# Loading K and V of four heads of B: one DMA of 128 partitions in place of four DMAs of 32

## The chip, the cores and the metric

The kernel runs on one core of a Trainium2 chip. The metric is device time in microseconds (us). Before: 829.31 us, median of 3 runs (829.16 to 829.46). Runs of a kernel on one core are called fast when they are within 1.5% of its fastest; every time and ratio below is of fast runs unless it says otherwise.

## The reference

Two attention problems, A and B, each with one query token, 32 heads of 128 channels and a cache of 16,384 keys in bf16. A attends to all keys; B only to the last 4,096. Both outputs go through an output projection and are concatenated. The code below is B's part, shortened.

```python
def _B_ref(x, k_cache, v_cache, wq, wo):        # A is the same with all Sk keys
    # ...
    W = min(4096, max(256, Sk // 4))
    q = ((x @ wq).reshape(B, Sq, Hq, Dh)).transpose(0, 2, 1, 3)
    k = k_cache[:, :, Sk - W:, :]                # one KV head per query head
    v = v_cache[:, :, Sk - W:, :]
    p = softmax(einsum("bhqd,bhkd->bhqk", q, k) * Dh ** -0.5)
    return einsum("bhqk,bhkd->bhqd", p, v) ... @ wo
```

A head of A has 4 MiB of K and 4 MiB of V. A head of B has 1 MiB of each, so four heads of B make a load as large as one of A. In device memory the heads of B's caches lie 4 MiB apart, since the cache holds all 16,384 keys.

## The kernel before

The unit of work is one head of A or four heads of B: 128 partitions of 128 keys each. In a unit of B, partition p holds keys of head p mod 4; the query and a mask are laid out to match. VectorE multiplies K by the query and adds halves, TensorE finishes the sum over channels and then applies the probabilities to V. Two K buffers and two V buffers are filled by DMAs that SyncE issues in one fixed order; a load is issued as soon as the last reader of its buffer is done. (Cuts are marked `# ...`.)

```python
cx.kt_pool = pool("kt", 2)
cx.vt_pool = pool("vt", 2)
# ...
units = []
for h in range(stA.H):
    units.append((stA, [h]))                               # one head of A
    if h % G == G - 1:
        units.append((stB, list(range(h - G + 1, h + 1)))) # four heads of B

def _load_kv(nc, cx, unit, which):
    pool, tag = (cx.kt_pool, "kt") if which == "k" else (cx.vt_pool, "vt")
    t = pool.tile([P, unit.keys, DH], BF16, tag=tag, name=tag)
    setattr(unit, tag, t)
    st = unit.st
    view = st.k_view if which == "k" else st.v_view
    n = len(unit.heads)                                    # 1 for A, 4 for B
    for g, h in enumerate(unit.heads):
        src = view[h].rearrange("(p l) d -> p l d", p=P // n)
        cx.o(nc.sync.dma_start(out=t[g:P:n, :, :], in_=src))
# ...
    if ch.last_of_unit:
        cx.loads.release("kt")      # after the multiply; V is released after its last matmul
```

The softmax here doesn't subtract the row's maximum and nothing guards it: scores larger than these inputs give would overflow.

Of the kernel before, what the change touches and what calls it, by code (L numbers as in the profile page):

```python
# [10 lines left out]
P = 128  # L11
# [132 lines left out]
# [5 lines that stand above are left out]
    st = unit.st  # L149
    view = st.k_view if which == "k" else st.v_view  # L150
    n = len(unit.heads)
    for g, h in enumerate(unit.heads):
        src = view[h].rearrange("(p l) d -> p l d", p=P // n)
        cx.o(nc.sync.dma_start(out=t[g:P:n, :, :], in_=src))  # L154


def _mult(nc, cx, ch):
# [160 lines left out]
def kernel(  # L318
# [144 lines left out]
    for i in range(n + 1):  # L463
        if i == G - 1:
            ld.add("kt", lambda: _load_wq(nc, cx, stB, "kt"))
        if i < n:
            ld.add("kt", lambda u=units[i]: _load_kv(nc, cx, u, "k"))
        if i:
            ld.add("vt", lambda u=units[i - 1]: _load_kv(nc, cx, u, "v"))
# [94 lines left out]
```

## Time and profile before

| | before |
|---|---|
| time, median | 829.31 us |
| span of the profiled execution | 827.4 us |
| bytes through the load queue | 352.33 MB |
| load queue, share of 16 engines | 99.2% |
| DVE, PE busy | 71%, 49% |
| packets under 512 B | 2,482 |
| issue of B's loads on SyncE | 64 issues, 0.587 us each (median) |

The span is the time of the profiled execution on the chip. In the views DVE is VectorE, PE is TensorE, SP is SyncE, and SPq is SyncE's own instruction queue, where it issues DMAs and waits. A packet is one piece that one DMA engine moves: here 10,496 of them are rows of 32 KB, and most of those under 512 B (2,226 of 2,482) are of 4 bytes, 9 ns each. They are called completions here: they come 16 to a DMA, as do the updates of the semaphore (the counter that reports a landing) of 139 of the 141 DMAs in the trace.

The first lines are from the page of the kernel before. "DMA" is the busy share of the 16 DMA engines in each of 40 slices of the span, in tenths; "GB/s" is what they moved in each slice; the line beginning q1 is the queue that carries all the loads.

```profile
DMA  9999999999999999999999999999999999999996
GB/s 380 437 430 432 433 430 432 431 431 432 431 429 436 432 430 430 431 433 433 432 429 430 429 431 432 432 432 430 431 430 430 429 431 432 431 432 433 431 423 290
DMA packets 13902, 352.69 MB, mean 426 GB/s; under 512 B 2482, under 2 KB 2484, under 8 KB 2868
...
q1 hardware_dynamic: 13588, 352.33, 99.2%
```

The engines never pause (99.2% busy), and they move 429 to 437 GB/s in every slice except the first and the last two. Slices with loads of B look like slices with loads of A. That is the main reading: this kernel waits for bytes. The median of the 40 slices is 431 GB/s.

Next, the chain of work that ended last, by engine and by line (shares of the span):

```profile
DMA 68%; DVE 20%; issue 9%; PE 1%; SPq 1%; ACT 0%; DVEq 0%
```

And the DMA issues of the loads (tile, source, engine and instruction, count, size of each, median us from issue to landing), from the same page:

```profile
kt<-in_A_k_cache_dram SPq DMA_DIRECT2D x32, 4096.0 KB, 27.1
...
kt<-in_B_k_cache_dram SPq DMA_DIRECT2D x32, 1024.0 KB, 23.7
vt<-in_B_v_cache_dram SPq DMA_DIRECT2D x32, 1024.0 KB, 22.5
```

4,096 KB take 9.7 us to move, yet 27.1 us pass from issue to landing. The difference, some 17 us, is mostly the queue of loads that stands in front. The timeline of SyncE shows how much of its time a load of B takes (start, duration, line, tile and source, count):

```profile
269.24 2.39 SPq L154 DMA_DIRECT2D kt<-in_B_k_cache_dram  x4
276.63 0.34 SPq L154 DMA_DIRECT2D vt<-in_A_v_cache_dram  x1
288.66 0.33 SPq L154 DMA_DIRECT2D kt<-in_A_k_cache_dram  x1
```

The trace also holds one record per DMA packet, with its start, its duration and its size. Cutting those records at every 4 MiB of landed bytes gives the time of each load while the queue is full; this table is worked out from them (medians, the first five and last few loads left out):

| us per 4 MiB | A, K | A, V | B, K | B, V |
|---|---|---|---|---|
| before | 9.716 | 9.719 | 9.727 | 9.726 |

### The profile page before, as it was taken

The numbers are of one execution on the slowest core, as the hardware profiler recorded it, in microseconds if no ns is written. First come the engines' busy times: TensorE is split into PE (matmuls) and PEld (weight loads), VectorE is DVE, ScalarE is ACT, GpSimd is POOL, SyncE is SP. The second block draws the span as 40 slices with busy tenths as digits, with TensorE's granted clock in tenths as the row PEclk, the third lists the DMA queues.
The fourth block names the chain that finished last, engine by engine and source line by source line (L and its number), as shares of the span: only waits on it lengthen the run. The fifth ranks groups of instructions, "written<-read, shape, count | busy, mean of one in ns | idle before, by whom it ended". The sixth has DMA issues, their size and how long they took to land.

```text
span 827.4 us, 5769 instructions
## 1 busy us (share of the span) xinstructions
PE 403.7 (49%) x2368; PEld 138.7 (17%) x2368; DVE 584.7 (71%) x286; ACT 68.1 (8%) x301; POOL 4.5 (1%) x17
## 2 busy tenths in 40 slices
PE   3356444434555544554454445445455455544355
PEld 1112111111211111211121111111111111211123
DVE  2892777777777777766777777777777776777760
ACT  2000011000100001000110001100010000100010
POOL 2000000000000000000000000000000000000000
PEclk9778677666776668766686666766677766676779
DMA  9999999999999999999999999999999999999996
GB/s 380 437 430 432 433 430 432 431 431 432 431 429 436 432 430 430 431 433 433 432 429 430 429 431 432 432 432 430 431 430 430 429 431 432 431 432 433 431 423 290
DMA packets 13902, 352.69 MB, mean 426 GB/s; under 512 B 2482, under 2 KB 2484, under 8 KB 2868
## 3 DMA queue, kind: packets, MB, share of 16 engines
q1 hardware_dynamic: 13588, 352.33, 99.2%
q8 instruction: 18, 0.29, 0.1%
q14 instruction: 8, 0.07, 0.0%
q10 hardware_dynamic: 288, 0.00, 0.0%
HBM read 352.32 MB, written 0.00 MB: 426 GB/s over the span
## 4 chain that ended last, share of the span: by engine, by line
DMA 68%; DVE 20%; issue 9%; PE 1%; SPq 1%; ACT 0%; DVEq 0%
DMA kt<-in_A_k_cache_dram 49%; DVE prod L161 12%; DMA kt<-in_B_k_cache_dram 12%; DVE half L173 6%; DMA wq_t<-in_B_wq_dram 3%; DMA woB<-in_B_wo_dram 3%; DMA vt<-in_B_v_cache_dram 2%; DVE sc L203 2%; SPq L154 1%; PE q_ps L123 1%; PE red L186 0%; PE acc L233 0%; ACT qallB L130 0%; DVEq L161 0%; DVE recip L267 0%
## 5 line engine op out<-in xcount | busy, mean ns | idle before, releaser
L186 PE MATMUL red<-half,ident 128*128 128x512 bf16 x640 | 253.3, 567 | 388.1 <-DVE half L173 374.4
L161 DVE TENSOR_TENSOR prod<-kt,qallA 128x8192 bf16<-128x8192 bf16 x64 | 283.2, 4426 | 159.8 <-DMA kt<-in_A_k_cache_dram 159.1
L173 DVE TENSOR_TENSOR half<-prod 128x4096 bf16<-128x4096 bf16 x80 | 182.5, 2282 | 0.0
L186 PEld LDWEIGHTS <-ident 128*128 128x128 bf16 x640 | 81.8, 128 | 535.3 <-issue 508.1
L161 DVE TENSOR_TENSOR prod<-kt,qallB 128x8192 bf16<-128x8192 bf16 x16 | 70.8, 4426 | 40.3 <-DMA kt<-in_B_k_cache_dram 40.1
L233 PE MATMUL acc<-vt,pA 128*16 128x512 bf16 x1024 | 89.4, 484 | 0.1
L210 ACT ACTIVATE pA<-sc 128x64 bf16<-128x64 f32 x64 | 16.4, 256 | 518.3 <-DVE sc L203 518.3
L203 DVE TENSOR_REDUCE sc<-red 128x64 f32<-128x512 f32 x80 | 54.7, 684 | 3.4 <-PE red L186 3.3
L233 PEld LDWEIGHTS <-pA 128*16 128x16 bf16 x1024 | 22.9, 100 | 73.2 <-issue 66.8
L210 ACT ACTIVATE p_sb<-sc,off 128x64 bf16<-128x64 f32 x64 | 21.5, 336 | 92.1 <-DVE sc L203 92.1
L257 PE MATMUL f_ps<-acc_sb,sel 128*4 128x128 f32 x128 | 16.6, 273 | 10.7 <-ACT acc_sb L244 10.7
L233 PE MATMUL acc<-vt,p_sb 128*16 128x512 bf16 x256 | 20.5, 450 | 0.2 <-DMA vt<-in_B_v_cache_dram 0.2
L244 ACT COPY acc_sb<-acc 128x512 f32<-128x512 f32 x16 | 9.4, 585 | 79.3 <-PE acc L233 79.3
L123 PE MATMUL q_ps<-wq_t,xbA 128*128 128x512 bf16 x32 | 8.5, 431 | 13.2 <-DMA wq_t<-in_A_wq_dram 13.2
L257 PEld LDWEIGHTS f_ps<-acc_sb,sel 128*4 128x4 f32 x128 | 9.8, 86 | 14.5 <-ACT acc_sb L244 12.3
L210 ACT ACTIVATION_READ_ACCUMULATOR pA<-sc 128x1 f32 x64 | 11.9, 187 | 0.0
L210 ACT ACTIVATION_READ_ACCUMULATOR p_sb<-sc,off 128x1 f32 x64 | 11.9, 187 | 0.0
L123 PE MATMUL q_ps<-wq_t,xbB 128*128 128x512 bf16 x32 | 7.2, 379 | 2.3 <-DMA wq_t<-in_B_wq_dram 1.6
L233 PEld LDWEIGHTS <-p_sb 128*16 128x16 bf16 x256 | 5.4, 95 | 15.6 <-issue 13.1
L269 ACT ACTIVATE orow<-f_ps,recip 4x128 bf16<-4x128 f32 x16 | 5.7, 358 | 20.5 <-DVE recip L267 20.5
L95 DVE COPY xbB<-xTB 128x32 bf16<-128x32 bf16 x16 | 1.5, 199 | 8.1 <-DMA xTB<-in_B_x_dram 8.1
L267 DVE RECIPROCAL recip<-f_ps 4x1 f32<-4x1 f32 x16 | 2.4, 150 | 6.0 <-PE f_ps L257 6.0
(35 smaller groups left out, 53.6 us busy)
## 6 DMA issues: line engine op xcount, KB each, us to landing
kt<-in_A_k_cache_dram SPq DMA_DIRECT2D x32, 4096.0 KB, 27.1
vt<-in_A_v_cache_dram SPq DMA_DIRECT2D x32, 4096.0 KB, 29.6
kt<-in_B_k_cache_dram SPq DMA_DIRECT2D x32, 1024.0 KB, 23.7
vt<-in_B_v_cache_dram SPq DMA_DIRECT2D x32, 1024.0 KB, 22.5
wq_t<-in_A_wq_dram SPq DMA_DIRECT2D x1, 4096.0 KB, 12.4
wq_t<-in_B_wq_dram SPq DMA_DIRECT2D x1, 4096.0 KB, 23.8
woA<-in_A_wo_dram SPq DMA_DIRECT2D x2, 2048.0 KB, 29.3
woB<-in_B_wo_dram SPq DMA_DIRECT2D x1, 2048.0 KB, 23.6
```

The costliest lines, as they stand in the source:

```text
L123: cx.o(nc.tensor.matmul(q_ps[:, :], lhsT=st.xb[:, c, g, :], rhs=w[:, g, j * (512 // DH) : (j + 1) * (512 // DH), :], start=(g == 0 and c = ...
L154: cx.o(nc.sync.dma_start(out=t[g:P:n, :, :], in_=src))
L161: cx.o(nc.vector.tensor_tensor(out=ch.prod[:, :, :], in0=u.kt[:, ch.k0 : ch.k0 + U, :], in1=q.rearrange("p (o d) -> p o d", o=1).broadcast ...
L173: cx.o(nc.vector.tensor_tensor(out=ch.half[:, :, :], in0=ch.prod[:, :, 0 : DH // 2], in1=ch.prod[:, :, DH // 2 : DH], op=ALU.add,))
L186: cx.o(nc.tensor.matmul(ch.red[:, :, :], lhsT=cx.ident[:, :], rhs=ch.half[:, :, b * W : (b + 1) * W], start=(b == 0), stop=(b == nb - 1),))
L203: cx.o(nc.vector.tensor_reduce(out=sc[:, :], in_=ch.red[:, :, :], axis=AX.X, op=ALU.add))
L210: cx.o(nc.scalar.activation(out=ch.p[:, :, g, :], in_=sc[:, :].rearrange("p (t e) -> p t e", e=4), func=ACT.Exp, scale=SCALE, bias=0.0 if ...
L233: cx.o(nc.tensor.matmul(gr.acc[r : r + 4 * G, :], lhsT=ch.p[:, t, :, :], rhs=u.vt[:, k : k + 4, :], start=(first and t < 4), stop=(last an ...
L244: cx.o(nc.scalar.copy(gr.acc_sb[:, :], gr.acc[:, :]))
L257: cx.o(nc.tensor.matmul(gr.f_ps[:, 0:DH], lhsT=cx.sel[:, e, :], rhs=gr.acc_sb[:, e * DH : (e + 1) * DH], start=False, stop=(e == 3), skip_ ...
L267: cx.o(nc.vector.reciprocal(recip[:, :], gr.f_ps[:, DH : DH + 1]))
L269: cx.o(nc.scalar.activation(out=gr.orow[:, :], in_=gr.f_ps[:, 0:DH], func=ACT.Copy, scale=recip[:, 0:1]))
```

## The change

The intent is one large DMA over 128 partitions in place of several small ones, with fewer issues on SyncE and fewer completions on the engines. The destination is the same tile in the same layout. The source becomes three-dimensional: 32 blocks of 32 KB, for each block the 4 heads, 4 MiB apart.

```diff
-    for g, h in enumerate(unit.heads):
-        src = view[h].rearrange("(p l) d -> p l d", p=P // n)
-        cx.o(nc.sync.dma_start(out=t[g:P:n, :, :], in_=src))
+    src = view[unit.heads[0] : unit.heads[0] + n].rearrange("g (i l) d -> i g l d", i=P // n)
+    cx.o(nc.sync.dma_start(out=t[:, :, :], in_=src[:, 0, :, :] if n == 1 else src))
```

## The prediction

> **What bounds the kernel now.** The DMA engines, by bytes. The page's queue table has the load queue busy for 99.2% of 16 engines' span (827.4 us), moving 352.33 MB; the slices show about 430 GB/s throughout. The chain of waits is 68% DMA; DVE is busy 71%, PE 49%. In the trace's packet records nearly everything is a 32 KB packet, one partition row of a load (10,496 of them): median 1.215 us. Priced at the shortest, 1.213 us, all bytes take 815 us on 16 engines. The first packet starts 2.0 us into the span, the last ends 1.4 us before its end. So a rearrangement of loads can win under 9 us (about 1%), and most of that is the start and the end.
>
> **Are the B loads slower now?** No. Cutting the packet records at every 4 MiB, a whole-head load of A takes 9.71 to 9.72 us (median), a four-DMA load of B 9.726 us: 0.01 us more, for 16 loads, so 0.2 us in the kernel.
>
> **What the change removes.** 64 DMAs become 16. Packets under 512 B are 2,482 now; 16 per DMA are completion writes, so 48 x 16 = 768 go, leaving about 1,714. One is 9 ns: 768 x 9 / 16 = 0.43 us at most. On SyncE, four issues take 2.39 us in the timeline, one about 0.33 to 0.6 us; but from issue to landing a load takes 27 us (median) for 9.7 us of transfer, so some 17 us of other loads stand in front, and an earlier issue only stands longer in the queue. Bytes, row length, buffers, and the order of work on PE, DVE and ACT stay.
>
> **What it adds or moves.** The DRAM side gets three dimensions: 32 blocks of 32 KB, 4 heads 4 MiB apart. [...]
>
> **On the critical path:** 0.2 to 0.4 us.
>
> **Predicted time:** 829.0 us, 827.0 to 832.0 us eight times in ten. Faster by over 2%: 0.01. Within 2%: 0.94. Slower by over 2%: 0.05.
>
> **What would show it.** Right: 32 KB packets still 10,496 with median 1.215 us; packets under 512 B near 1,714; load queue at 99%; GB/s slices level; B loads at 9.71 to 9.73 us per 4 MiB; from issue to landing of B's loads 25 to 29 us; fewer issues on SyncE.
>
> **What would make it wrong.** (1) The source is cut differently: shorter packets, or unequal rows per engine, seen as more packets or slices dipping where B is loaded. (2) [...] 32 KB packets above 1.3 us. B's loads are 67 of 352 MB, about 156 us, so packets 10% longer cost 16 us, twice as long 156 us. (3) Issuing the new form takes SyncE over 10 us and drains the queue. Nothing I see makes it faster by 2%: the bytes forbid it.

0.2 to 0.4 us off the 829.31 us before came to 829.0 us. The 16 and 156 us under (2) are estimates from the 156 us that B's loads take.

## The result

| | before | after |
|---|---|---|
| time, median of 6 | 829.26 us (829.05 to 829.46) | 829.13 us (828.85 to 829.23) |
| ratio after to before | | 0.9998, 95% interval 0.9985 to 1.0011 |
| load queue, share | 99.2% | 99.1% |
| packets under 512 B | 2,482 | 1,714 |
| SyncE issues of B's loads | 64 of 0.587 us | 16 of 0.547 us |
| DVE idle for K of B | 40.1 us | 39.9 us |

Ratios here are the mean time of one kernel's fast runs over the mean of the other's of the same rounds, so they are not quite the ratio of the medians. The time is the same. The lines of the page after that answer to those of before:

```profile
DMA  9999999999999999999999999999999999999996
GB/s 380 434 430 432 432 432 435 431 432 430 434 429 434 430 431 430 434 431 426 434 432 430 429 431 430 431 432 432 432 430 431 429 431 433 431 433 431 432 423 285
DMA packets 13133, 352.68 MB, mean 426 GB/s; under 512 B 1714, under 2 KB 1716, under 8 KB 2100
...
q1 hardware_dynamic: 12820, 352.33, 99.1%
```

Exactly 768 packets are gone, 16 for each of the 48 DMAs saved. Bytes and rate are the same. What VectorE waited for K of B (us, times), before and then after:

```profile
  DMA kt<-in_B_k_cache_dram: 40.1, 8
```

```profile
  DMA kt<-in_B_k_cache_dram: 39.9, 8
```

The DMA issues after:

```profile
kt<-in_A_k_cache_dram SPq DMA_DIRECT2D x32, 4096.0 KB, 27.0
...
kt<-in_B_k_cache_dram SPq DMA_DIRECT2D x8, 4096.0 KB, 27.0
vt<-in_B_v_cache_dram SPq DMA_DIRECT2D x8, 4096.0 KB, 29.6
```

A reader could take 27.0 us after 23.7 us for a loss. It is not: before, the figure is the median of four pieces of 1 MiB, after, it is of the whole 4 MiB. What VectorE waited for K of B in all, 40.1 and 39.9 us, hardly changed.

SyncE's timeline around the same load shows the saving, 0.55 us in place of 2.39:

```profile
269.33 0.55 SPq L153 DMA_DIRECT2D kt<-in_B_k_cache_dram  x1
276.70 0.34 SPq L153 DMA_DIRECT2D vt<-in_A_v_cache_dram  x1
288.75 0.33 SPq L153 DMA_DIRECT2D kt<-in_A_k_cache_dram  x1
```

The next two issues start 0.07 and 0.09 us later than before, not 1.84 us earlier. SyncE's own waits say why. First the kernel before, then after (who waited for what, us in total, times, longest):

```profile
SPq L154 <- DVE prod L161: 417.1, 37, 12.0
SPq L154 <- PE acc L233: 221.6, 36, 7.9
```

```profile
SPq L153 <- DVE prod L160: 428.9, 37, 11.8
SPq L153 <- PE acc L232: 235.0, 36, 7.9
```

SyncE spends 16 x 1.84 = 29.4 us less on issuing and 11.8 + 13.4 = 25.2 us more on waiting for buffers. The time saved on issues became waiting.

Per 4 MiB, from the packet records, A's loads take 9.715 to 9.716 us, B's 9.712 (K) and 9.713 (V). By these medians B's loads gained 0.015 and 0.013 us each, 0.22 us for all 16; by the means of the same loads they gained 0.007 and 0.005 us, 0.1 us in all. Both are within the scatter of the run times.

### The profile page after: what moved, and what is told of

Same layout as the page of the kernel before. It is cut to its first block, busy times and chain, and to the rows that moved or that the text cites. A ratio compares the mean times of both kernels' runs of the same rounds, so it can differ in the third digit from the quotient of the medians.

```text
span 827.4 us, 5697 instructions
## 1 busy us (share of the span) xinstructions
PE 402.1 (49%) x2368; PEld 139.4 (17%) x2368; DVE 584.8 (71%) x286; ACT 68.2 (8%) x301; POOL 4.6 (1%) x17
## 2 busy tenths in 40 slices
DMA packets 13133, 352.68 MB, mean 426 GB/s; under 512 B 1714, under 2 KB 1716, under 8 KB 2100
## 3 DMA queue, kind: packets, MB, share of 16 engines
q1 hardware_dynamic: 12820, 352.33, 99.1%
## 4 chain that ended last, share of the span: by engine, by line
DMA 69%; DVE 20%; issue 10%; SPq 0%; DVEq 0%; PE 0%
DMA kt<-in_A_k_cache_dram 53%; DMA kt<-in_B_k_cache_dram 13%; DVE prod L160 12%; DVE half L172 6%; DMA woB<-in_B_wo_dram 3%; DVE sc L202 2%; SPq L141 0%; DVE recip L266 0%; DVEq L160 0%; PE out L302 0%; SPq L107 0%; DVE rowB L311 0%
## 5 line engine op out<-in xcount | busy, mean ns | idle before, releaser
L160 DVE TENSOR_TENSOR prod<-kt,qallB 128x8192 bf16<-128x8192 bf16 x16 | 70.8, 4426 | 40.2 <-DMA kt<-in_B_k_cache_dram 39.9
L232 PE MATMUL acc<-vt,pA 128*16 128x512 bf16 x1024 | 87.2, 474 | 2.0 <-DMA vt<-in_A_v_cache_dram 2.0
## 6 DMA issues: line engine op xcount, KB each, us to landing
vt<-in_A_v_cache_dram SPq DMA_DIRECT2D x32, 4096.0 KB, 29.6
vt<-in_B_v_cache_dram SPq DMA_DIRECT2D x8, 4096.0 KB, 29.6
```

Source lines behind the costliest of these rows:

```text
L160: cx.o(nc.vector.tensor_tensor(out=ch.prod[:, :, :], in0=u.kt[:, ch.k0 : ch.k0 + U, :], in1=q.rearrange("p (o d) -> p o d", o=1).broadcast ...
L232: cx.o(nc.tensor.matmul(gr.acc[r : r + 4 * G, :], lhsT=ch.p[:, t, :, :], rhs=u.vt[:, k : k + 4, :], start=(first and t < 4), stop=(last an ...
```

## The experiments

The theory: the queue is full all the time, so the time is the bytes; a DMA more or less costs some nanoseconds of completions, and its issue is hidden. The rivals: each DMA carries a fixed cost of its own; or the issue is hidden only by the backlog of loads; or the number of DMAs never matters. Two further questions: on how many engines a load finishes when another dimension is the slowest, and whether rows 4 MiB apart cost time.

a_split4, b_twice and the two onebuf runs shared one chip; the b_pieces runs, b_cols8, heads_outer and pitch4m a second; b_more_bytes, pitch4m_pad and heads_outer_pad a third. Each is compared with the kernel before on its own chip.

### a_split4: the change undone four times over

```diff
-    for g, h in enumerate(unit.heads):
-        src = view[h].rearrange("(p l) d -> p l d", p=P // n)
-        cx.o(nc.sync.dma_start(out=t[g:P:n, :, :], in_=src))
+    for g in range(G):
+        src = view[unit.heads[g] if n > 1 else unit.heads[0]]
+        src = src.rearrange("(p l) d -> p l d", p=P // n)
+        cx.o(nc.sync.dma_start(out=t[g:P:G, :, :], in_=src if n > 1 else src[g:P:G]))
```

> The kernel before with the 64 whole-head loads of A cut into four DMAs of 32 partitions as well: the change undone four times over, 192 more DMAs, same bytes and rows. Theory (a DMA costs the engines only its 16 completion packets; issue and completion delay are hidden): from 9.726 against 9.713 us per 4 MiB, 0.0043 us per extra DMA, so +0.8 us, at 9 ns per packet at most +1.7 us: 829.3 to 831.5 us, ratio to before 1.000 to 1.003. SyncE then issues a load in 2.4 us, still below 9.71 us of transfer. [...] Packets under 512 B: 2482 + 3072 = about 5554.

Measured: 830.0 us (829.91 to 830.06, 5 runs) against 829.12 us; ratio 1.0009 (0.9995 to 1.0023); 5,554 packets under 512 B:

```profile
DMA packets 16975, 352.72 MB, mean 426 GB/s; under 512 B 5554, under 2 KB 5556, under 8 KB 5940
```

The difference of the medians, 0.88 us over 192 DMAs, is 4.6 ns for each; the interval of the ratio includes no change at all. In the packet records A's loads now take 9.726 us per 4 MiB, what B's took before, where they took 9.716. A fixed cost in series of more than about 10 ns is ruled out: the upper end of the interval, 0.23% or 1.9 us, is 9.9 ns for each of the 192 DMAs (an estimate from the interval).

### onebuf_four and onebuf_one: both kernels without a backlog

Both kernels with one K and one V buffer; the output weights get a place of their own in both, so that the single K buffer suffices.

```diff
-    cx.kt_pool = pool("kt", 2)
-    cx.vt_pool = pool("vt", 2)
+    cx.kt_pool = pool("kt", 1)
+    cx.vt_pool = pool("vt", 1)
-    ld.free = {"kt": 2, "vt": 2}
+    ld.free = {"kt": 1, "vt": 1}
```

> The kernel before with one K buffer and one V buffer in place of two (and the output weights in a place of their own): a load is issued only when the last reader is done, so no backlog stands ahead of it. Near 1000 us (950 to 1150), queue share well under 90%. To be set against the run onebuf_one. Theory: a 1 MB piece takes 2.4 us to move and its issue 0.59 us, so pieces follow each other without a gap even when the queue is empty: the two differ by under 5 us in all. Rival A (only the backlog of 17 us hides the 1.8 us of extra issue): four pieces slower by 15 to 30 us. [...]

> The changed kernel with one K buffer and one V buffer. Near 1000 us; theory: within 5 us of onebuf_four, B loads landing in the same time from issue of the first piece. Rival A: faster than onebuf_four by 15 to 30 us[...].

Measured: onebuf_four 1052.43 us (1047.90 to 1054.69), onebuf_one 1053.37 us (1051.05 to 1055.62). The one with fewer DMAs is, if anything, 0.9 us slower, inside the scatter. The first fence is onebuf_four, the second onebuf_one: the load queue's line, and what VectorE waited for K of B (us, times).

```profile
q1 hardware_dynamic: 13588, 352.33, 80.1%
...
  DMA kt<-in_B_k_cache_dram: 80.9, 8
```

```profile
q1 hardware_dynamic: 12820, 352.33, 79.9%
...
  DMA kt<-in_B_k_cache_dram: 79.7, 8
```

The queue stands empty a fifth of the time, and a load of B still costs VectorE 10.1 us in four pieces and 10.0 in one. The packet records say for which loads this tests the point: at each of the eight issues of K of B, in both kernels, the queue had been empty for about 2.5 us, whereas V of B is issued while the K load before it still moves, except the last. So for K the backlog is not what makes the four issues harmless. A piece of 1 MiB moves in 2.4 us and is issued in about 0.6; the next piece is always there in time.

### b_more_bytes and b_twice: are the bytes the bound?

```diff
     cx.o(nc.sync.dma_start(out=t[:, :, :], in_=src[:, 0, :, :] if n == 1 else src))
+    if n > 1:
+        m = 24
+        spare = cx.singles.tile([P, m, DH], BF16, tag=f"spare{which}", name=f"spare{which}")
+        cx.o(nc.sync.dma_start(out=spare[:, :, :], in_=src[:, :, 0:m, :]))
```

> The changed kernel with one more DMA after each load of B, of 24 of its 128 keys into a spare tile that nobody reads (b_twice had to wait for its first write; this one waits for nothing): 16 DMAs of 128 rows of 6 KB, 12.6 MB. Theory (the queue is full, every byte shows): 6 KB packets between 0.159 and 0.312 us, so 0.236 x 8 x 16 = +30 us: 857 to 861 us. Rival (there is slack under other work): under 850 us.

Measured: 859.4 us (859.29 to 859.49) against 829.41 us, so +30.0 us, where the packets were to cost 30.2 (0.236 x 8 x 16). The queue's share is as before:

```profile
q1 hardware_dynamic: 15124, 364.91, 99.2%
```

The added bytes show in the time in full; there is no slack behind which a load could hide.

An earlier try, b_twice, issued each load of B twice into the same tile:

```diff
-    cx.o(nc.sync.dma_start(out=t[:, :, :], in_=src[:, 0, :, :] if n == 1 else src))
+    for _ in range(1 if n == 1 else 2):
+        cx.o(nc.sync.dma_start(out=t[:, :, :], in_=src[:, 0, :, :] if n == 1 else src))
```

> The changed kernel with each load of B issued twice into the same tile: 67.1 MB more through the queue, no other work more. Theory (the queue is full all the time, so every byte shows at the rate of a 4 MiB load): 16 x 9.71 = +155 us, 984 us (980 to 990 if the second write may follow the first at once; a wait for the first landing would add more). Rival (compute or waits share the bound, 19% of the chain is DVE): part of it would be absorbed, below 950 us.

Measured: 1042.0 us, 213 us more in place of 155. It is a miss of design: the second write had to wait for the first to land, and SyncE waited with it, as its waits show:

```profile
SPq L154 <- DMA vt<-in_B_v_cache_dram: 380.5, 15, 40.6
SPq L154 <- DMA kt<-in_B_k_cache_dram: 204.9, 8, 28.0
```

The queue's share fell to 94.3%. This run doesn't price bytes; b_more_bytes does.

### b_pieces16, b_pieces32 and b_cols8: how small may a piece be?

In the kernel before, B's four pieces are cut along the keys too, into 4 (b_pieces16) or 8 (b_pieces32) parts:

```diff
+    m = 1 if n == 1 else 8                       # 4 in b_pieces16
+    w = unit.keys // m
     for g, h in enumerate(unit.heads):
         src = view[h].rearrange("(p l) d -> p l d", p=P // n)
-        cx.o(nc.sync.dma_start(out=t[g:P:n, :, :], in_=src))
+        for j in range(m):
+            s = slice(j * w, (j + 1) * w)
+            cx.o(nc.sync.dma_start(out=t[g:P:n, s, :], in_=src[:, s, :]))
```

b_cols8 is the control with the same short rows as b_pieces32 but pieces of 128 partitions, cut from the changed kernel:

```diff
-    cx.o(nc.sync.dma_start(out=t[:, :, :], in_=src[:, 0, :, :] if n == 1 else src))
+    m = 1 if n == 1 else 8
+    w = unit.keys // m
+    for j in range(m):
+        s = slice(j * w, (j + 1) * w)
+        cx.o(nc.sync.dma_start(out=t[:, s, :], in_=src[:, 0, s, :] if n == 1 else src[:, :, s, :]))
```

> Each load of B in 16 DMAs: 32 partitions, 8 KB rows, 256 KB each (before has 4 of 1 MB). Theory: the change was free because 1 MB moves in 2.4 us and is issued in 0.59 us; the knee is where a piece moves as fast as it is issued, 0.59 us x 432 GB/s = 255 KB. At the knee: +3 us for 8 KB packets (0.309 us against 0.303), +1 us for completions, and little idle: 832 to 845 us. [...] Rival (number of DMAs never matters): 833 us.

> Each load of B in 32 DMAs: 32 partitions, 4 KB rows, 128 KB each, half the knee. The program has eight DMA semaphores in rotation, so a piece waits until the eighth piece before it has landed and SyncE can't run far ahead. Theory: issue bound, 32 x 0.59 = 18.9 us per B load in place of 9.7: +9 us x 16 = +145 us less what the backlog still hides (at most 8 pieces, 4.7 us per load), plus 8 us for 4 KB packets: 900 to 1000 us, with the slices of GB/s dipping where B is loaded. Rival (completions and packet size alone): 829 + 7.6 + 2 = 839 us, the same as the run b_cols8.

> Control for the last: the same 4 KB rows, but 8 DMAs of 128 partitions (512 KB each) per load of B. Theory: packets cost 159 against 152 ns per 4 KB, +7.6 us, and 512 KB is above the knee of 255 KB, so nothing else: 834 to 840 us.

| run | pieces of a B load | time | ratio to before (95%) |
|---|---|---|---|
| before | 4 of 1 MiB, 32 KB rows | 829.28 us | |
| b_cols8 | 8 of 512 KB, 4 KB rows | 837.49 us | 1.0100 (1.0085 to 1.0115) |
| b_pieces16 | 16 of 256 KB, 8 KB rows | 850.26 us | 1.0244 (1.0222 to 1.0266) |
| b_pieces32 | 32 of 128 KB, 4 KB rows | 986.96 us | 1.1901 (1.1876 to 1.1925) |

b_cols8 came within 0.6 us of what its packets alone should cost (+8.2 measured, +7.6 expected). b_pieces32 has the same rows, in 32 DMAs of 32 partitions in place of 8 of 128, and is 149 us slower; the row length is not the cause. That it is the number of DMAs, and not their 32 partitions, shows in the rate of issue. The timeline of SyncE in b_pieces32, and the stretches of one load of K of B (bounds, length, busy time of PE, PEld, DVE, ACT and POOL with the number of instructions, granted TensorE clock, share of the DMA engines, GB/s):

```profile
329.88 12.23 SPq L158 DMA_DIRECT2D kt<-in_B_k_cache_dram  x19
```

```profile
305.00:315.00 10.00, 7.20 (x42) 2.26 (x43) 6.30 (x3) 0.35 (x2) 0.00 (x0) 0.71 0.98 423
...
333.00:342.00 9.00, 2.28 (x19) 0.47 (x18) 0.40 (x1) 0.00 (x0) 0.00 (x0) 0.69 0.68 206
```

19 issues in 12.23 us are 0.644 us for each, and 131,072 bytes per 0.644 us are 204 GB/s: the 206 GB/s of that stretch. SyncE's issuing has become the bound. The backlog can't help, since a piece waits until the eighth DMA before it has landed. The built program gives its DMAs eight semaphores in turn: in the trace of the kernel before, all 141 issues take them in strict rotation, none starts before the landing of the eighth before it, and three start 16 or 17 ns after that landing. SyncE waited 185.4 us on K of A and 131.4 us on V of A in b_pieces32, where the kernel before waited 36.9 and 9.6.

b_pieces16 was to take 832 to 845 us and took 850. With 0.644 us per issue in place of the 0.59 that I used, 256 KB come at 407 GB/s, under the 432 GB/s that slices of the kernel before show: the knee lies near 272 KB (an estimate, 0.644 us x 432 GB/s), so that 256 KB is already past it. That explains only part of the miss: 16 issues take 10.3 us, but in the packet records, cut as above, a load of B takes 11.2 us per 4 MiB. One stretch of a load of K of B:

```profile
295.00:300.00 5.00, 3.19 (x8) 0.99 (x7) 1.76 (x1) 0.00 (x0) 0.00 (x0) 0.66 0.95 315
```

The queue's share over the whole run stayed at 99.0% while slices dipped to 386 GB/s; the 8 KB packets there took 0.333 us in the mean, for 0.309 at the median. Why the records book the shortfall mostly as longer packets and not as idle engines, and with it the rest of the miss, stays open.

### heads_outer: the head as the slowest dimension

```diff
-    src = view[unit.heads[0] : unit.heads[0] + n].rearrange("g (i l) d -> i g l d", i=P // n)
+    src = view[unit.heads[0] : unit.heads[0] + n].rearrange("g (i l) d -> g i l d", i=P // n)
```

The lines that lay out the query and the mask to match (partition p holds head p div 32), and the index for heads of A, are left out here. The result is right.

> The changed kernel with the head as the slowest dimension of the source (4 heads x 32 blocks in place of 32 blocks x 4 heads); masks are changed to match, the result stays right. [...] Theory: 32 KB packets unchanged at 1.215 us, but a load of B takes 32 of them in a row on 4 engines: 38.9 us for 9.7, +29 us x 16 = up to +466 us, less what A's rows on the other 12 engines overlap: 1100 to 1300 us. Rival (the engine is chosen by the SBUF partition, the order in DRAM plays no part): 829 us.

Measured: 1817.64 us (1805.31 to 1830.21), ratio 2.1914. That is far outside the expected range, so the theory holds in part only. The packets under 512 B and two stretches of the trace:

```profile
DMA packets 12941, 352.68 MB, mean 193 GB/s; under 512 B 1522, under 2 KB 1524, under 8 KB 1908
```

```profile
560.00:570.00 10.00, 5.17 (x40) 1.65 (x40) 2.20 (x2) 0.35 (x2) 0.00 (x0) 0.83 1.00 205
590.00:600.00 10.00, 0.00 (x0) 0.00 (x0) 0.00 (x0) 0.00 (x0) 0.00 (x0) 0.50 0.25 85
```

1,522 packets are 192 fewer than after: 12 for each of 16 loads. So a load of B has 4 completions in place of 16, and the stretch from 590 us shows a quarter of the engines busy (share 0.25, 85 GB/s): with the 4 heads as the slowest dimension it moves on 4 engines. But in the stretch from 560 us all engines are busy and move half the usual rate, 205 GB/s; the packet records have 4,563 of 10,496 packets of 32 KB over 1.58 us, more than the 2,048 packets that B has. Those are what the estimate lacked.

### pitch4m and pitch4m_pad: 16 heads 4 MiB apart in one load

pitch4m takes 16 heads x 8 blocks as one load, so that the slowest dimension is 16 heads, 4 MiB apart (the result is wrong; bytes, rows and work are the same). pitch4m_pad changes the distance to 4 MiB + 4 KiB (its line for the start, `at`, is left out; it keeps the reads inside the cache).

```diff
+        src = view[16 * (gi // 4) : 16 * (gi // 4) + 16].rearrange("h (b l) d -> h b l d", b=P // n)
+        src = src[:, 8 * (gi % 4) : 8 * (gi % 4) + 8, :, :]
     # pitch4m_pad: the same sizes, but the heads 2097152 + 2048 elements apart
+        src = bass.AP(tensor=view.tensor, offset=at,
+                      ap=[[2097152 + 2048, 16], [16384, P // 16], [DH, unit.keys], [1, DH]])
```

> The changed kernel with a load of B taken as 16 heads x 8 blocks of 32 KB[...] (wrong result on purpose: B's heads are mixed; same bytes, same rows, same work). [...] packets of B's loads 2.4 us in place of 1.215, +155 us, 985 us[...]. Rival (for 32 KB rows read by one core the distance plays no part): 829 us, packets 1.215 us.

> The run pitch4m with one number changed: heads read 4 MiB + 4 KiB apart in place of 4 MiB (wrong result on purpose, other rows of the same heads); SBUF side, row size, engines and issue the same to the letter. Two causes are open for its 2.5 us packets: (memory) sixteen engines reading at exact distances of 4 MiB at the same time[...]. Memory: packets of B's loads back to 1.215 us, 828 to 833 us. Port: packets 2.5 us and 1130 to 1150 us as before.

Measured: pitch4m 1143.75 us (1135.89 to 1148.00), ratio 1.3806; pitch4m_pad 1146.60 us (1142.10 to 1150.73), ratio 1.3822. One load of B in each, pitch4m first:

```profile
255.00:265.00 10.00, 0.96 (x8) 0.63 (x9) 7.24 (x4) 1.43 (x8) 0.00 (x0) 0.74 1.02 216
285.00:295.00 10.00, 0.95 (x3) 0.40 (x3) 8.23 (x5) 0.71 (x3) 0.00 (x0) 0.61 0.99 426
```

```profile
255.00:265.00 10.00, 1.67 (x24) 0.99 (x17) 3.76 (x1) 0.59 (x1) 0.00 (x0) 0.79 1.00 210
285.00:295.00 10.00, 2.89 (x32) 1.44 (x31) 4.39 (x2) 0.59 (x1) 0.00 (x0) 0.83 1.01 431
```

All 16 engines are busy in a load of B (share 1.0, and 1,714 packets under 512 B as after), but at half the rate, 216 and 210 GB/s; in the packet records a 32 KB packet takes 2.5 us there and 1.22 in the next load of A. 4 KiB more of distance changes nothing. So the exact distance of 4 MiB alone is not the cause, and my expectation of pitch4m, which rested its 2.4 us on that distance, had the right packet time for a reason that fell: that was luck. Its sum of +155 us, twice the packet time of B's loads, stands as an estimate from their 9.71 us each. That total was wrong: it came to +314 us. The queue's share of 91.6% leaves some engines idle (some 95 us, an estimate: 8.4% of the span of 1134 us), and 2,784 packets over 1.58 us show that packets beyond B's 2,048 are slow as well.

The second of the two causes named in the expectation of pitch4m_pad, called "port" there, is cut from it: no run here shows which engine wrote which partition. What the runs show is that the loads of 16 heads x 8 blocks moved at half rate, and those of the changed kernel, 32 blocks x 4 heads, at the full one (32 KB packets of 1.215 us at the median). Why is open.

### heads_outer_pad: the same question for heads_outer

The edit is that of heads_outer with the heads 4 MiB + 4 KiB apart, as above.

> The run heads_outer with heads 4 MiB + 4 KiB apart (wrong result on purpose). heads_outer took 1818 us where four engines alone should give at most 829 + 466 = 1295; its trace has stretches with 4 engines busy and packets of 1.22 us, and others with 16 engines busy and packets of 2.5 us. If the distance of 4 MiB is behind the 2.5 us packets: 1200 to 1320 us and few packets over 1.6 us. If it is something of loads on 4 engines beside loads on 16: 1750 to 1850 us, with 2.5 us packets as before.

Measured: 1722.91, 1770.78, 1815.75 and 1873.19 us. The scatter is so wide that only the first counts as a fast run, and no ratio is given. In the trace of that run 4,645 packets of 32 KB took over 1.58 us, about as many as in heads_outer. Here too the exact distance alone is not the cause. What slows these packets, which are more than B's 2,048, is open.

## Why the prediction was right

- **The time.** 829.0 us was predicted, 827.0 to 832.0; measured 829.13. The forecast of no visible change, at 94%, held.
- **The bound is bytes.** Shown: the queue at 99.1% after, and 12.6 MB more cost 30.0 us (b_more_bytes).
- **B's loads were not slow before.** Shown: 9.727 and 9.726 us per 4 MiB became 9.712 and 9.713. The predicted 0.2 us of gain is there in the medians of the packet records (0.22 us; 0.1 us by the means); the run times, with an interval of about 0.13% either way, can't show it.
- **Packets.** Predicted 10,496 packets of 32 KB at a median of 1.215 us and about 1,714 under 512 B; both came exactly.
- **The landing.** Predicted 25 to 29 us from issue; K took 27.0, V 29.6, a little outside. V of A takes 29.6 as well; I had taken the range from K.
- **The reason why issues don't matter was too narrow.** The prediction said that "an earlier issue only stands longer in the queue". For the load itself it does: in the load of the timelines the last of the four pieces was issued about 1.8 us after the first, yet VectorE started on that K at 296.65 us before and at 296.47 after. The loads that follow are not issued earlier at all: SyncE waits for their buffers, 25.2 us more for 29.4 us saved. But K of B has no such backlog in onebuf_four and onebuf_one, and these are equal too. The stronger reason is the ratio of 2.4 us of transfer to about 0.6 us of issue for each piece, and b_cols8 and the pieces runs show where it ends, between 512 KB and 256 KB.
- **The engines of a load.** Shown: 16 completions per load of B after, with 32 blocks outermost, and 4 with the 4 heads outermost (heads_outer, share of the engines 0.25).
- **Rows 4 MiB apart.** The prediction expected no cost. Shown: none in the changed kernel (32 KB packets at 1.215 us, as before). With 16 heads outermost, 4 MiB apart, the rate was halved (2.5 us), and a distance of 4 KiB more did not heal it. What makes the difference is open.

The experiments point to no version that beats both kernels. At the shortest packet time (1.213 us for 32 KB), all bytes take 815 us on 16 engines, against a span of 827.4 us.

## What to carry to other kernels

Before merging DMAs, see whether the queue is already full and whether a piece moves longer than it takes to issue: here 1 MiB pieces at 2.4 us against 0.6 us cost nothing, with or without a backlog, and merging them won nothing. The number of DMAs begins to matter where bytes per issue fall under issue time times rate, here near 272 KB by estimate (0.644 us x 432 GB/s); measured, 512 KB pieces cost nothing beyond their packets, and 256 KB pieces 2.4%. When a merge makes the DRAM side three-dimensional, look at which dimension becomes the slowest and how many rows each of its slices has: the same bytes to the same tile took 829 us with 32 slices of 4 rows, and 1144 us with 16 slices of 8 and 1818 us with 4 slices of 32 (the 16-slice run read other heads, so the slices are not shown to be its cause).
